# A hand-ordered transformer block on one core is replaced by one with a planned order, in which VectorE computes part of the softmax exponentials as sums of shifted bit patterns

## The chip, the cores and the metric

The kernel runs on one core of one Trainium2 chip. The metric is the device time of one execution in microseconds, the median over the runs. Engines are called as in the profile: PE (TensorE), ACT (ScalarE), DVE (VectorE), POOL (GpSimd) and SP (SyncE, which issues DMAs).

## The reference

One block on x of 2048 tokens and width D = 640, in bf16. `mod` is silu(c) times a matrix, cut into six vectors sa, ca, ga, sb, cb, gb.

```python
h = _layernorm(x) * (1 + ca) + sa
qkv = (h @ wqkv).reshape(B, S, 3, H, Dh)          # H = 32 heads, Dh = 20
scores = einsum('bhqd,bhkd->bhqk', q, k) * Dh ** (-0.5)
x = x + ga * ((softmax(scores) @ v) @ wo)
h = _layernorm(x) * (1 + cb) + sb
x = x + gb * (((h @ w_gate) * (h @ w_up)) @ w_down)   # inner width 1536
```

A unit below is the scores of one head for 128 keys and 512 queries, one 128x512 tile in a PSUM bank. There are 32 heads x 16 key tiles x 4 chunks of 512 queries = 2048 units.

## The kernel before

**Start** (lines 512 to 871). Modulation vectors are computed by matmuls, the layer norm of the four groups of 512 tokens runs on DVE with a square root on ACT, transposes on PE give hT, and ACT applies scale and shift while it evicts (L620). For each group the first half of V and the K of the first four heads are projected (`v_round`, `k_or_q_round`, evicted by DVE at L752 and L734). The other projections are left to rounds that are put between attention steps.

**Attention** (lines 1099 to 1221). Heads go in sets of three (ten sets, and one of two). An item is a chunk of queries with a set of heads, and has 16 steps, one for each key tile. A step is: one matmul of scores for each head, in the 32 rows of PE that hold that head (L1130); one exponential on ACT over all of them, 128x1536, into `Pbuf` (L1146); one PV matmul for each head, in its own 32 columns of PE (L1159), which sums over the 16 steps into PSUM bank 6. Column 0 of V is 1, so the sum of the exponentials comes out as a row of its own. Scores use two sets of three banks in turn, so the scores of step g + 2 wait for the exponential of step g. At the end of an item DVE transposes the sums (L1183), takes the reciprocal (L1187), multiplies (L1189) and transposes back into `Oc` (L1193). The next item's first PV waits for L1183.

**Order.** It is written by hand in a loop over 704 steps: exponential g, scores g + 2, PV g, and then `xs.inject(g)`, which puts a few matmuls of the waiting round (a projection or a piece of a suffix) behind them, up to a budget of time, into bank 7. Where there is none it puts a matmul that nobody reads (L852).

**Suffix** (`suffix_task`, from L915). For each chunk: out-projection over 11 sets of heads (L959) and the residual (L968), layer norm (L980 to L992), transposes (L999), gate and up projections (L1036, L1049) with DVE's product (L1054), the scaling of w_down by gb (L934), the down projection (L1073) and the result (L1083), stored by SP. The first three suffixes lie between the attention steps of the next chunks, and the fourth is the tail.

Of the kernel before, what the change touches and what calls it, by code (L numbers as in the profile page):

```python
# [4 lines left out]
ACT = mybir.ActivationFunctionType  # L5
# [4 lines left out]
F32R = mybir.dt.float32r  # L10

ENGS = ("sp", "act", "pe", "dve", "pool")


class Ev:
    __slots__ = ("ctr", "val", "step")

    def __init__(self, ctr, val, step=-10 ** 6):
        self.ctr = ctr
        self.val = val  # L20
        self.step = step


class Ctr:

    def __init__(self, prog, name, step=1):
        self.prog = prog
        self.name = name
        self.sem = prog.nc.alloc_semaphore(name)
        self.step = step  # L30
        self.n = 0
        self.owner = None


class EngProg:
    def __init__(self, prog, key):
        self.prog = prog
        self.key = key
        self.ops = []
        self.waited = {}  # L40

    def wait(self, *evs):
        for ev in evs:
            if ev is None:
                continue
            ctr = ev.ctr
            if ev.val > self.waited.get(ctr.name, 0):
                self.waited[ctr.name] = ev.val
                sem, val = ctr.sem, ev.val
                self.ops.append(lambda e, sem=sem, val=val: e.wait_ge(sem, val))  # L50

    def ins(self, fn, inc=None, waits=()):
        for ev in waits:
            self.wait(ev)
        ev = None
        if inc is not None:
            if inc.owner is None:
                inc.owner = self.key
            assert inc.owner == self.key, f"counter {inc.name} owned by {inc.owner}, used by {self.key}"
            inc.n += inc.step  # L60
            ev = Ev(inc, inc.n, self.prog.cur_step)
            sem, step = inc.sem, inc.step
            self.ops.append(lambda e, fn=fn, sem=sem, step=step: fn(e).then_inc(sem, step))
        else:
            self.ops.append(lambda e, fn=fn: fn(e))
        return ev


class Prog:
    def __init__(self, nc):  # L70
        self.nc = nc
        self.engs = {k: EngProg(self, k) for k in ENGS}
        self.ctrs = {}
        self.cur_step = -10 ** 6

    def ctr(self, name, step=1):
        assert name not in self.ctrs
        c = Ctr(self, name, step)
        self.ctrs[name] = c
        return c  # L80

    def __getitem__(self, k):
        return self.engs[k]

    def dgrp(self, name):
        return DmaGrp(self, name)

    def emit(self):
        nc = self.nc
        with nc.Block() as block:  # L90

            @block.sync
            def _(e):
                for f in self.engs["sp"].ops:
                    f(e)

            @block.scalar
            def _(e):
                for f in self.engs["act"].ops:
                    f(e)  # L100

            @block.tensor
            def _(e):
                for f in self.engs["pe"].ops:
                    f(e)

            @block.vector
            def _(e):
                for f in self.engs["dve"].ops:
                    f(e)  # L110

            @block.gpsimd
            def _(e):
                for f in self.engs["pool"].ops:
                    f(e)


class DmaGrp:

    def __init__(self, prog, name):  # L120
        self.prog = prog
        self.ctr = prog.ctr(name, 16)
        self.closed = False

    def dma(self, eng, fn, waits=()):
        assert not self.closed, "DMA group already closed"
        if self.ctr.owner is None:
            self.ctr.owner = eng.key
        assert self.ctr.owner == eng.key, "DMA group must use a single engine/queue"
        eng.ins(fn, inc=self.ctr, waits=waits)  # L130

    def done(self):
        self.closed = True
        return Ev(self.ctr, self.ctr.n)


class Arena:

    def __init__(self, nc, base, top):
        self.nc = nc  # L140
        self.base = base
        self.top = top
        self.cur = base
        self.peak = base
        self.count = 0

    def alloc(self, name, shape, dtype, align=64):
        size = 1
        for s in shape[1:]:
            size *= s  # L150
        size *= mybir.dt.size(dtype)
        off = (self.cur + align - 1) // align * align
        assert off + size <= self.top, f"SBUF overflow allocating {name} ({size} B at {off}, top {self.top})"
        self.count += 1
        t = self.nc.alloc_sbuf_tensor_at(f"{name}_{self.count}", list(shape), dtype, offset=off, align_bytes=32)
        self.cur = off + size
        self.peak = max(self.peak, self.cur)
        return t

    def mark(self):  # L160
        return self.cur

    def reset(self, m):
        self.cur = m

class Banks:

    def __init__(self, banks):
        self.banks = list(banks)
        self.free_ev = {b: None for b in self.banks}
        self.i = 0

    def next(self):
        b = self.banks[self.i % len(self.banks)]
        self.i += 1
        return b, self.free_ev[b]

    def release(self, b, ev):
        self.free_ev[b] = ev

    def set_all(self, ev):
        for b in self.banks:
            self.free_ev[b] = ev


class XRound:

    def __init__(self, mms, after, first_waits=(), name="", lag=2):
        self.mms = mms
        self.after = after
        self.first_waits = list(first_waits)
        self.name = name
        self.lag = lag

    def ready(self, step):
        for w in self.first_waits:
            ev = w() if callable(w) else w  # L200
            if ev is None:
                if callable(w):
                    return False
                continue
            if ev.step + self.lag > step:
                return False
        return True


class XTask:  # L210
    def __init__(self, name, ready_step, gen, budget=450):
        self.name = name
        self.ready_step = ready_step
        self.gen = gen
        self.done = False
        self.buf = None
        self.budget = budget

    def peek(self):
        if self.buf is None and not self.done:  # L220
            try:
                self.buf = next(self.gen)
            except StopIteration:
                self.done = True
        return self.buf

    def pop(self):
        r = self.peek()
        self.buf = None
        return r  # L230


class XSched:

    def __init__(self, pe, c_pe, banks, xbank):
        self.pe = pe
        self.c_pe = c_pe
        self.banks = banks
        self.xbank = xbank
        self.tasks = []  # L240
        self.cur = None
        self.round_end_step = -10
        self.no_start_until = -10
        self.xbank_free = None
        self.mode = "attn"
        self.stats = {"steps": 0, "mm": 0, "idle_steps": 0}
        self.filler = None
        self.filler_waits = []

    def add_task(self, task):  # L250
        self.tasks.append(task)

    def _head(self, step):
        while self.tasks:
            t = self.tasks[0]
            if step is not None and step < t.ready_step:
                return None
            if t.peek() is None and t.done:
                self.tasks.pop(0)
                continue  # L260
            return t
        return None

    def _issue_mm(self, rnd, i, bank, is_first):
        cost, fn = rnd.mms[i]
        last = (i == len(rnd.mms) - 1)
        waits = []
        if is_first:
            waits = [w() if callable(w) else w for w in rnd.first_waits]
            if self.mode == "attn":  # L270
                waits.append(self.xbank_free)
            else:
                waits.append(self.banks.free_ev[bank])
        ev = self.pe.ins(lambda e, fn=fn, bank=bank: fn(e, bank), inc=(self.c_pe if last else None), waits=waits)
        self.stats["mm"] += 1
        return ev, last
# [116 lines left out]
def build_kernel(nc, A_x, A_wqkv, A_wo, B_x, B_w_gate, B_w_up, B_w_down, c, w_mod, out,  # L393
# [4 lines left out]
    H = 32  # L398
# [889 lines left out]
```

## Time and profile before

| what | value |
|---|---|
| median of three runs | 1135.11 us (1135.11 to 1136.35) |
| span of the profiled execution | 1138.6 us |
| mean granted clock of PE | 0.913 of full speed |
| ACT busy | 969.7 us, 752 instructions |
| PE busy | 952.1 us, 6035 matmuls |
| DVE busy | 390.4 us, 690 instructions |

Rows of groups read: line, engine, operation, output and inputs, shapes, number; then busy time in us and mean length in ns; then the idle time of the engine before them and what ended it. Rows of a timeline begin with start and length in us, rows of the chain of waits too. Rows of stretches give the stretch, its length, the busy time of PE, PE's weight loads, DVE, ACT and POOL with numbers of instructions, the granted clock, the busy share of the DMA engines and GB/s.

### The profile page before, as it was taken

What the parts mean: (1) busy time and instruction counts of PE and PEld (TensorE: products, weight loads), DVE (VectorE), ACT (ScalarE), POOL (GpSimd) and SP (SyncE); (2) the same over time, 40 slices, a digit from 0 to 9 for tenths busy, and PEclk for the clock granted to TensorE, in tenths of its full rate; (3) what the DMA queues carried; (4) which work ended last, traced back from release to release, by engine and by line L of the source; (5) the groups of instructions that cost most, each with busy time, mean ns of one, the idle gap of its engine ahead of it and who ended that gap; (6) DMA issues with size and microseconds to landing.
All of it is one profiled execution on the core that took longest, in us unless ns stands there. A gap on an engine that the chain in (4) does not pass through costs nothing.

```text
span 1138.6 us, 14720 instructions
## 1 busy us (share of the span) xinstructions
PE 952.1 (84%) x6035; PEld 293.7 (26%) x6095; DVE 390.4 (34%) x690; ACT 969.7 (85%) x752; POOL 37.8 (3%) x52
## 2 busy tenths in 40 slices
PE   1677898899998888888997898889987888889778
PEld 0331222222222222222322222223222222223434
DVE  2741322344323333332114333321123333322475
ACT  1559999999999899999999999999987999999200
POOL 7000000000000000000000000000000000000000
PEclk9788999999989889898989779999977899989889
DMA  8100001000022001100230011100400011100422
GB/s 295 57 1 1 1 1 30 1 1 1 1 75 53 1 12 45 37 13 6 68 78 1 1 30 41 35 1 18 133 1 1 12 36 35 24 6 20 126 64 64
DMA packets 80418, 40.59 MB, mean 36 GB/s; under 512 B 64544, under 2 KB 80032, under 8 KB 80352
## 3 DMA queue, kind: packets, MB, share of 16 engines
q1 hardware_dynamic: 77328, 32.29, 11.0%
q10 hardware_dynamic: 2624, 4.92, 1.2%
q0 software_dynamic: 400, 2.46, 0.6%
q8 instruction: 48, 0.79, 0.3%
q14 instruction: 18, 0.15, 0.0%
HBM read 37.03 MB, written 2.62 MB: 35 GB/s over the span
## 4 chain that ended last, share of the span: by engine, by line
PE 39%; ACT 29%; issue 16%; DVE 13%; POOL 2%; another core or an unknown queue 0%; ACTq 0%; POOLq 0%
ACT Pbuf L1146 26%; PE ps_all L1159 9%; PE ps_all L1130 9%; PE ps_all L724 7%; PE ps_all L959 3%; PE ps_all L1036 3%; PE ps_all L1073 3%; PE ps_all L1049 2%; PE ps_all L746 2%; DVE OT L1183 2%; DVE KT_sb L734 1%; DVE QT_sb L734 1%; ACT hT L620 1%; PE ps_all L852 1%; DVE xn L990 1%
## 5 line engine op out<-in xcount | busy, mean ns | idle before, releaser
L1146 ACT ACTIVATE Pbuf<-ps_all 128x1536 bf16<-128x1536 f32 (+1 forms) x704 | 928.9, 1526 | 40.6 <-PE ps_all L1130 39.4
L1130 PE MATMUL ps_all<-QT_sb,KT_sb 32*128 32x512 bf16 x2048 | 296.1, 412 | 73.1 <-ACT Pbuf L1146 49.5
L1159 PE MATMUL ps_all<-Pbuf,V_sb 128*24 128x512 bf16 x2048 | 294.1, 412 | 9.0 <-DVE OT L1183 8.8
L1130 PEld LDWEIGHTS ps_all<-QT_sb,KT_sb 32*128 32x128 bf16 x2048 | 68.9, 92 | 323.7 <-ACT Pbuf L1146 244.2
L1159 PEld LDWEIGHTS ps_all<-Pbuf,V_sb 128*24 128x24 bf16 x2048 | 67.2, 89 | 189.4 <-issue 169.0
L959 PE MATMUL ps_all<-wo_sb,Oc 128*128 128x320 bf16 x352 | 76.7, 344 | 13.9 <-DVE h2T L1005 11.7
L1036 PE MATMUL ps_all<-h2T,wgst 128*128 128x512 bf16 x216 | 71.9, 410 | 9.8 <-DVE hprod L1054 4.4
L1073 PE MATMUL ps_all<-wd_sb,hprod 128*128 128x320 bf16 x384 | 72.5, 313 | 6.2 <-DVE wd_sb L934 5.4
L1049 PE MATMUL ps_all<-h2T,wust 128*128 128x512 bf16 x228 | 71.8, 398 | 4.9 <-DVE gsb L1041 3.4
L1183 DVE STREAM_TRANSPOSE OT<-ps_all 96x512 f32<-96x512 f32 (+1 forms) x44 | 31.3, 711 | 118.3 <-PE ps_all L1159 118.3
L1041 DVE COPY gsb<-ps_all 128x512 f32<-128x512 f32 x48 | 32.9, 685 | 89.8 <-PE ps_all L1036 82.4
L1054 DVE TENSOR_TENSOR hprod<-ps_all,gsb 128x512 bf16<-128x512 f32 x48 | 32.8, 684 | 89.9 <-PE ps_all L1049 78.8
L968 DVE TENSOR_TENSOR xck<-ps_all,xck 128x320 bf16<-128x320 f32 x32 | 15.3, 486 | 121.5 <-PE ps_all L959 121.5
L746 PE MATMUL ps_all<-Wv,hT 128*128 128x384 bf16 x160 | 40.6, 394 | 12.9 <-ACT hT L620 12.9
L1083 DVE TENSOR_TENSOR xck<-ps_all,xck 128x320 bf16<-128x320 f32 x32 | 15.5, 484 | 98.5 <-PE ps_all L1073 98.5
L724 PE MATMUL ps_all<-hT,Wk 128*128 128x512 bf16 x147 | 43.5, 394 | 6.3 <-DVE KT_sb L734 2.9
L724 PE MATMUL ps_all<-hT,Wq 128*128 128x512 bf16 x149 | 42.8, 383 | 5.3 <-issue 1.0
L734 DVE CAST KT_sb<-ps_all 128x512 bf16<-128x512 f32 x32 | 22.1, 691 | 67.1 <-PE ps_all L724 67.1
L959 PEld LDWEIGHTS ps_all<-wo_sb,Oc 128*128 128x128 bf16 x352 | 29.2, 106 | 51.8 <-issue 22.7
L734 DVE CAST QT_sb<-ps_all 128x512 bf16<-128x512 f32 x32 | 22.1, 692 | 56.0 <-PE ps_all L724 53.9
L1073 PEld LDWEIGHTS ps_all<-wd_sb,hprod 128*128 128x128 bf16 x384 | 30.3, 99 | 38.4 <-issue 17.9
L934 DVE TENSOR_TENSOR wd_sb<-wd_sb,mods_b 128x640 bf16<-128x640 bf16 x48 | 39.0, 813 | 0.0
(68 smaller groups left out, 433.5 us busy)
## 6 DMA issues: line engine op xcount, KB each, us to landing
wd_sb<-in_B_w_down_dram SPq DMA_DIRECT2D x4, 1920.0 KB, 9.4
wgst<-in_B_w_gate_dram SPq DMA_DIRECT2D x48, 160.0 KB, 2.7
wust<-in_B_w_up_dram SPq DMA_DIRECT2D x48, 160.0 KB, 2.8
wmod_sb<-in_w_mod_dram ACTq DMA_DIRECT2D x4, 1200.0 KB, 13.9
x<-in_A_x_dram SPq DMA_DIRECT2D x4, 640.0 KB, 7.1
xck<-in_A_x_dram SPq DMA_DIRECT2D x4, 640.0 KB, 4.3
out_dram<-xck SPq DMA_DIRECT2D x16, 160.0 KB, 1.8
wraw<-in_A_wqkv_dram POOLq DMA_DIRECT2D x5, 480.0 KB, 5.9
```

The lines of the kernel that those rows point to most:

```text
L724: fn = lambda e, b, kt=kt: e.matmul(psbank(b), Wx[:, kt, sg, :], hT[:, tc, kt, :], start=(kt == 0), stop=(kt == KT - 1))
L734: eve = dve.ins(lambda e: e.tensor_copy(dst[:, sg, tc * 512:(tc + 1) * 512], psbank(b)), inc=c_ev, waits=w)
L746: fn = lambda e, b, kt=kt: e.matmul(psbank(b)[:, 0:ncol], hT[:, tc, kt, (t % 4) * 128:(t % 4 + 1) * 128], Wv[:, kt, cc * ncol:(cc + 1) * n ...
L934: ev_wdp_l[0] = dve.ins(lambda e: e.tensor_tensor(wd_sb[:, fc, :], wd_sb[:, fc, :], mods_b[:, 2, :], ALU.mult), inc=c_ev, waits=[ev_wdl])
L959: fn = lambda e, b, j=j, tl=tl, nch=nch: e.matmul(ps_all[:, b, 0:320], Ocq[:, j, tl * 128:(tl + 1) * 128], wo_sb[:, j, nch * 320:(nch + 1) ...
L1036: fn = lambda e, b, kt=kt, stg=stg: e.matmul(psbank(b), wgst[:, stg, kt, :], h2T[:, kt, :], start=(kt == 0), stop=(kt == KT - 1))
L1049: fn = lambda e, b, kt=kt, stg=stg: e.matmul(psbank(b), wust[:, stg, kt, :], h2T[:, kt, :], start=(kt == 0), stop=(kt == KT - 1))
L1073: fn = lambda e, b, fc=fc, tl=tl, nch=nch: e.matmul(ps_all[:, b, 0:320], hprod[:, fc, tl * 128:(tl + 1) * 128], wd_sb[:, fc, nch * 320:(nc ...
L1130: fn = lambda e, bs=bs, i=i, sg=sg, s=s, cq=cq, kt=kt: e.matmul(ps_all[:, bs * 3 + i, :], KT_sb[32 * s:32 * s + 32, sg, kt * 128:(kt + 1) ...
L1146: fn = lambda e, sl=sl, nh=nh, bs=bs: e.activation(Pbuf[:, sl, 0:nh * 512], ps_sflat[bs][:, 0:nh * 512], ACT.Exp, scale=SCALE)
L1159: fn = lambda e, i=i, h=h, sl=sl, kt=kt: e.matmul(ps_all[32 * i:32 * i + VW, BO, :], V_sb[:, kt, h * VW:(h + 1) * VW], Pbuf[:, sl, i * 512 ...
L1183: ev_t1 = dve.ins(lambda e, rows=rows: e.transpose(OT[0:rows, :], ps_all[0:rows, BO, :]), inc=c_at, waits=[ev_pv[g], st["onorm"]] + extra)
```

## The change

The kernel is written anew. The program of each engine now comes from a planner (`Sched`) that runs when the kernel is built: each task has a duration, dependencies, a priority and buffer slots, the planner steps through a modelled time, and each engine's instructions stand in the order in which the planner started them. On the chip this order is fixed and only semaphores hold. The description calls it the same layout, but the kernel before has no such planner.

What is computed otherwise:

- Heads go in sets of four (8 sets), so an item has 64 units; 32 items in all. Scores use all four row groups of PE and PV all four column groups.
- ACT's units are cut into groups of three and two in turn, in banks 0 to 2 and 3 to 4. Banks 5 and 6 serve all other matmuls, bank 7 the PV sums.
- Of each item, 4 units in the first chunk and 8 in the others (`QUADS`) get no exponential on ACT. The queries are scaled at L750 so that a score is already 128 times the base-2 exponent. DVE adds a bias and clips at 0, written as int16 (L980); read as bf16, that is a piecewise linear exponential. Five more int16 tiles are made from it by adding a constant (L999, 2048 columns for four units). PE runs the PV matmul on each of the six tiles, so that their sum, with row sums that carry the same factor, stands for the exponential. The constants of ACT's exponential fit that factor.
- The start needs fewer modulation vectors: silu is computed with the exponential's table, and the two vectors of the first layer norm come as columns from 25 one-column matmuls each. Exponentials begin when the first keys are there. The out-projection packs the heads into 5 pieces of 128 rows, which SP copies together by DMA after each item (L1069). POOL scales wo and w_down.
- Where PE has little to do, the planner puts in matmuls that nobody reads (L1475).

The core of the diff:

```diff
+QUADS = [1, 2, 2, 2]
+SHIFTS = (0, 18, 34, 56, 77, 105)
...
-    SETS = [tuple(range(i, min(i + 3, H))) for i in range(0, H, 3)]
-    NSET = len(SETS)
-    VW = 24
+    NSET = 8
+    VW = DH + 1
...
+                u.is_d = q < nq and s == kg % 4
...
+        k = 3 if gi_ % 2 == 0 else 2
+        glist.append(ubuf[:k])
...
-        fn = lambda e, sl=sl, nh=nh, bs=bs: e.activation(Pbuf[:, sl, 0:nh * 512], ps_sflat[bs][:, 0:nh * 512],
-                                                         ACT.Exp, scale=SCALE)
-        ev_exp[g] = act.ins(fn, inc=c_exp, waits=waits)
+            return e.activation(pbuf[:, cellp["p"], 0:nu * 512],
+                                ps[:, b0:b0 + nu, :].rearrange("p b c -> p (b c)"), AFT.Exp, scale=ESCALE)
+        ta = Task("act", nu * 512 / 1.2 + 52.0, fexp, [ts], prio=g, name=f"E{g}")
...
+                return e.tensor_scalar(DB0[:, st_["slot"], x * 512:(x + 1) * 512], bank(cell["b"]), EBIAS, 0.0,
+                                       op0=ALU.add, op1=ALU.max)
...
+                return e.tensor_scalar(DSS[:, cell["s"], :], DB0[:, st_["slot"], :], float(SHIFTS[jj]), None, op0=ALU.add)
+            tsx = Task("dve", sb_cost(2048, .27), fsh, list(st_["p1"]) + wpad[("K", 1)] + wpad[("Q", 1)], prio=2.5 + .001 * qi, name=f"SH.{qi}.{jj}")
...
+                        srcf = lambda st_=st_, xx=xx: DB0[:, st_["slot"], xx * 512:(xx + 1) * 512].bitcast(BF16)
...
+                        srcf = lambda s_=st_["ss"][jj], xx=xx: DSS[:, s_, xx * 512:(xx + 1) * 512].bitcast(BF16)
...
+        d_xc = dma("sp", 128 * ntl * D * 2, lambda e: e.dma_start(xck[:, 0:ntl, :], xv[:, t0:t0 + ntl, :]),
+                   out_prev + proj_last, prio=15, gate=max(0, gb - 20))
```

How the order changes, at three places. PE, in the middle of an item of the second chunk, while the gate projection of the first is put between (QT and KT are queries and keys, Pbuf the exponentials, wgst the gate weights). Before:

```order
L1130 MATMUL ps_all<-QT_sb_86,KT_sb_85 128x512 x3
L1159 MATMUL ps_all<-Pbuf_78,V_sb_88 24x512 x3
L1036 MATMUL ps_all<-h2T_75,wgst_93 128x512
L1130 MATMUL ps_all<-QT_sb_86,KT_sb_85 128x512 x3
L1159 MATMUL ps_all<-Pbuf_78,V_sb_88 24x512 x3
L1049 MATMUL ps_all<-h2T_75,wust_94 128x512 x2
```

Now, in the last chunk (PA and PB are the exponentials of groups of three and two, DSS the shifted tiles, stg the gate and up weights):

```order
L919 MATMUL ps_all<-QT_73,KT_67 128x512 x3
L1307 MATMUL ps_all<-PA_78,Vf_77 21x512
L1307 MATMUL ps_all<-PA_78,Vf_77 32x512 x2
L1307 MATMUL ps_all<-DSS_81,Vf_77 32x512 x3
L1307 MATMUL ps_all<-DSS_81,Vf_77 21x512
L919 MATMUL ps_all<-QT_73,KT_67 128x512 x2
L1307 MATMUL ps_all<-PB_79,Vf_77 21x512
L1307 MATMUL ps_all<-PB_79,Vf_77 32x512
L1307 MATMUL ps_all<-DSS_81,Vf_77 32x512 x3
L1307 MATMUL ps_all<-DSS_81,Vf_77 21x512
L1191 MATMUL ps_all<-h2T_94,stg_99 128x512 x2
```

A phase of PV now holds the units of a group and four matmuls for one term of a quad, and a phase of PV or projections does not follow each phase of scores. DVE, at the end of an item with a suffix in the same stretch. Before (gsb and hprod are gate and product, OT to Oc the item's end):

```order
L1041 COPY gsb_76<-ps_all 128x512
L1183 STREAM_TRANSPOSE OT_79<-ps_all 96x512
L1187 RECIPROCAL invT_80<-OT_79 96x16
L1189 TENSOR_TENSOR OTn_81<-OT_79,invT_80 96x512
L1193 STREAM_TRANSPOSE Oc_35_83<-OTn_81 96x512
L1054 TENSOR_TENSOR hprod_77<-ps_all,gsb_76 128x512
L934 TENSOR_TENSOR wd_sb_92<-wd_sb_92,mods_b_53 128x640
```

Now:

```order
L1206 TENSOR_TENSOR hprod_93<-ps_all,gsb_101 128x512
L999 TENSOR_SCALAR DSS_81<-DB_32_80 128x2048
L1050 STREAM_TRANSPOSE OT_83<-ps_all 128x512
L999 TENSOR_SCALAR DSS_81<-DB_32_80 128x2048
L1053 RECIPROCAL invT_65<-OT_83 128x16
L999 TENSOR_SCALAR DSS_81<-DB_32_80 128x2048
L1055 TENSOR_TENSOR OTn_84<-OT_83,invT_65 128x512
L999 TENSOR_SCALAR DSS_81<-DB_32_80 128x2048
L1058 STREAM_TRANSPOSE OcT_85<-OTn_84 128x512
L999 TENSOR_SCALAR DSS_81<-DB_32_80 128x2048 x4
L980 TENSOR_SCALAR DB_32_80<-ps_all 128x512
```

The adds of 2048 columns stand between the steps of the item's end, and the scaling of w_down is gone from DVE. PE, behind the last exponentials (L1475 is read by nobody, wd and hprod belong to the third chunk, wo to the last). Before:

```order
L1159 MATMUL ps_all<-Pbuf_78,V_sb_88 24x512 x2
L852 MATMUL ps_all<-QT_sb_86,KT_sb_85 128x512
L959 MATMUL ps_all<-wo_sb_89,Oc_35_83 128x320 x44
L999 MATMUL ps_all<-ident_49,xn_22_70 128x128 x5
L959 MATMUL ps_all<-wo_sb_89,Oc_35_83 128x320 x22
```

Now:

```order
L1307 MATMUL ps_all<-PB_79,Vf_77 21x512
L1221 MATMUL ps_all<-wd_92,hprod_93 128x320 x74
L1475 MATMUL ps_all<-KT_67,ident_49 128x512 x12
L1119 MATMUL ps_all<-wo_98,Ocp_86 128x320 x40
L1475 MATMUL ps_all<-KT_67,ident_49 128x512 x6
L1151 MATMUL ps_all<-ident_49,xn_48_96 128x128 x20
```

The rest of the third chunk's down projection now stands between the last scores and the last out-projection, and the out-projection has 40 matmuls in one piece.

More of the change, by code (lines that the diff above doesn't have):

```diff
@@ L1 @@
 import math
+import heapq
 import concourse.bass as bass
 from concourse import mybir
-ACT = mybir.ActivationFunctionType
+AFT = mybir.ActivationFunctionType
 ALU = mybir.AluOpType
@@ L35 @@
[L35 to L44, printed above, removed]
-                continue
[L46 to L66, printed above, removed]
@@ L69 @@
[L69 to L115, printed above, removed]
@@ L118 @@
[L118 to L134, printed above, removed]
@@ L137 @@
[L137 to L164, printed above, removed]
@@ L210 @@
[L210 to L230, printed above, removed]
```

2261 lines of the change are left out of this document (1310 added, 951 removed).

## Prediction

> **What bounds the kernel now.** I read the page's head and slices, then the groups of instructions by form, then the timeline of the two ends and of one steady stretch, then the table of 40 us stretches.
>
> ```profile
> span 1138.6 us, 14720 instructions
> PE 952.1 (84%) x6035; PEld 293.7 (26%) x6095; DVE 390.4 (34%) x690; ACT 969.7 (85%) x752; POOL 37.8 (3%) x52
> ...
> PE   1677898899998888888997898889987888889778
> ...
> ACT  1559999999999899999999999999987999999200
> ```
>
> ScalarE (ACT) is full from the fourth slice to the 37th and empty at both ends; PE's 84% is pipelined matmuls with waits under them. The groups say what ACT does, and the timeline where it starts and stops:
>
> ```profile
> L1146 ACT ACTIVATE Pbuf<-ps_all 128x1536 bf16<-128x1536 f32 x640 | 869.6, 1570 | 37.5 <-PE ps_all L1130 36.7
> L1146 ACT ACTIVATE Pbuf<-ps_all 128x1024 bf16<-128x1024 f32 x64 | 61.4, 1093 | 3.1 <-PE ps_all L1130 2.7
> ```
>
> ```profile
> 91.41 4.13 ACT L1146 ACTIVATE Pbuf<-ps_all 128x1536 bf16<-128x1536 f32 x3
> ...
> 1029.67 31.24 ACT L1146 ACTIVATE Pbuf<-ps_all 128x1536 bf16<-128x1536 f32 x28
> ```
>
> The exponentials run from 91.4 to 1060.9 us. So the span is 91.4 of start, 969.5 of exponentials (931 busy by the two groups, 40.6 of waits for PE's scores) and 77.7 of tail. Inside the middle, PE keeps up:
>
> ```profile
> 500.49 0.39 PE L1130 MATMUL ps_all<-QT_sb,KT_sb 32*128 32x512 bf16 x3
> 500.81 0.39 PE L1159 MATMUL ps_all<-Pbuf,V_sb 128*24 128x512 bf16 x3
> 501.13 0.39 PE L1036 MATMUL ps_all<-h2T,wgst 128*128 128x512 bf16 x1
> 501.83 0.39 PE L1130 MATMUL ps_all<-QT_sb,KT_sb 32*128 32x512 bf16 x3 [0.31 <-ACT Pbuf L1146]
> ```
>
> ```profile
> 1099.18 1.08 PE ps_all L1036 x5
> 1122.66 13.21 PE ps_all L1073 x96
> ```
>
> One step is 1.34 us (500.49 to 501.83), ACT's pace. A phase of three tiled matmuls holds PE for 0.32 us. The last two rows, from the chain of waits in the tail, give 0.216 us for a 512-column matmul and 0.138 for a 320-column one; so 0.32 is one matmul time plus about 0.105 for the change of kind.
>
> **The exponentials.** The table QUADS takes 4 of 64 units in each of the eight items of the first chunk and 8 in the rest: 32 + 192 = 224 of 2048 units leave ACT, not an eighth. The order has 365 exponentials of three units, 364 of two and one of one. Priced by busy time per call (869.6/640 = 1.359, 61.4/64 = 0.959) they take 846 us. By distances from start to start, 1.34 above and 0.90 below, 818.
>
> The 0.90 is from the chain of waits, in the last item of two heads:
>
> ```profile
> 1055.24 0.69 ACT Pbuf L1146
> 1056.14 0.70 ACT Pbuf L1146
> ```
>
> I take 832 against 931: **99 us less**. One set of score banks is refilled while ACT reads the other; the shorter cover is now 0.9 us, which sufficed in the two-head steps of before (3.1 us of wait in 64).
>
> **The start.** Every item needs all 2048 keys. Before, projections of the four token groups came one after another, and no exponential ran until the first ones of all four were done. In the new order exponentials run on the keys at hand, and VectorE (DVE) sets when the last K tile of the first heads is there:
>
> ```profile
> L734 DVE CAST QT_sb<-ps_all 128x512 bf16<-128x512 f32 x32 | 22.1, 692 | 56.0 <-PE ps_all L724 53.9 <-remote 2.1
> L1083 DVE TENSOR_TENSOR xck<-ps_all,xck 128x320 bf16<-128x320 f32 x32 | 15.5, 484 | 98.5 <-PE ps_all L1073 98.5
> L568 DVE BATCH_NORM_STATS2 st<-x 128x6 f32<-128x320 bf16 x16 | 7.7, 483 | 11.2 <-DMA x<-in_A_x_dram 11.2
> L1005 DVE COPY h2T<-ps_all 128x640 bf16<-128x640 bf16 x16 | 7.8, 486 | 7.9 <-PE ps_all L999 7.9
> L988 DVE TENSOR_SCALAR xn<-xck,mv,rs 128x640 bf16<-128x640 bf16 x16 | 7.1, 446 | 16.0 <-POOL rs L985 16.0
> L1187 DVE RECIPROCAL invT<-OT 96x16 f32<-96x16 f32 x40 | 10.0, 249 | 1.4
> L690 ACT COPY Wk<-wraw 128x640 bf16<-128x640 bf16 x5 | 3.2, 724 | 7.8 <-DMA wraw<-in_A_wqkv_dram 7.8
> L934 DVE TENSOR_TENSOR wd_sb<-wd_sb,mods_b 128x640 bf16<-128x640 bf16 x48 | 39.0, 813 | 0.0
> ```
>
> Up to that K tile DVE's order holds 32 statistics x 0.483, 16 normalisations x 0.446, 18 evictions of transposes x 0.486, 12 of V x 0.484, 9 of 512 columns x 0.692, 5 shifts at 0.9 (below) and some 4 us of small ones: 52 us. The first x lands at 11.2 us as before; with about 5 us of waits for POOL and the modulation the tile is there at 68. The first exponential comes at about 33 us: x at 11.2, DVE's first statistics and normalisation 6, ACT's twelve copies of weights at 0.72 from 18 (L690's began at 30.3, behind 8.7 MB of loads; now some 5 MB lie ahead) to about 27, two projections of 2 and their evictions. By 68 us 44 of the first item's 60 ACT units can be done, 20 us of ACT at 0.456 a unit. So the start is worth 68 - 20 = 48 us instead of 91.4: **43 less** (between 36 and 51 less).
>
> **What is added to DVE.** Per four units: four evictions of 512 columns to int16 (0.692 each) and five adds over 2048 int16 columns. No row shows an int16 add in SBUF. Columns cost 1.08 ns and an instruction 0.14 us by the rows of 512 and 320 columns; L934's 640 columns fit that, the normalisation's 640 in 0.446 don't. With that row's rate and 0.14 fixed, 2048 columns take 1.1 us; with the small reciprocal's 0.249 as fixed cost, 0.9; at 1.08 ns a column, 2.35. I take 0.9, since the add has no per-partition operands to fetch: 10 adds and 8 evictions, 14.5 us per item, beside some 6 us of the item end, evictions and layer norm, about 20.5 of the 25.5 us in which ACT does 56 units. So DVE stays hidden.
>
> [...]
>
> **What is added to PE.** Six terms make 224 PV matmuls into 1344. Counted in the order: 3168 PV matmuls which, issued in order on four column groups, fill 951 slots x 0.216 = 205 us; 2048 scores in 183; 1812 others in 290 (K, V, out-projection use fewer or narrower matmuls: heads in fours, 21 columns of V, out-projection over 5 instead of 11 pieces); 1442 changes of kind x 0.105 = 151. That is 830; the same count of before, with 1992 changes, is 849. Longer PV phases thus pay for the six terms. Without tail (60) and what precedes the first score (5), 765 us lie beside some 890 us of exponentials and waits. PE is hidden at full clock, but tightly: in the first chunk it has as much work as ACT. So I take before's wait of 0.058 us a call (40.6/704) for 730 calls, 42, and 8 more for that chunk: **50**, between 15 and 110.
>
> ```profile
> 40.00:80.00 40.00, 27.02 (x164) 15.71 (x165) 24.46 (x67) 16.73 (x25) 2.41 (x1) 0.76 0.12 34
> 240.00:280.00 40.00, 36.83 (x243) 10.14 (x247) 19.44 (x29) 40.00 (x31) 0.00 (x0) 1.00 0.00 1
> 640.00:680.00 40.00, 35.04 (x201) 8.26 (x201) 13.40 (x23) 37.69 (x28) 0.79 (x2) 0.75 0.08 17
> ```
>
> ```profile
> core 0: 1138.6 us, clock 0.913
> ```
>
> The granted clock (third number from the end) is 1.00 where PE has projections between its phases and ACT is never idle, 0.75 where it has few. New PV phases are denser, so I expect at least 0.913, before's mean.
>
> **The tail.** SP stores the third chunk's output before it loads x for the last one into the same tile, and PE has 74 down-projections left when the last scores are gone.
>
> ```profile
> xck<-in_A_x_dram SPq DMA_DIRECT2D x4, 640.0 KB, 4.3
> out_dram<-xck SPq DMA_DIRECT2D x16, 160.0 KB, 1.8
> ```
>
> So: 1 for the last PV, 74 x 0.138 = 10.2, eviction 0.5, store 1.8, load 4.3: 17.8 us until the out-projection; the item end and its copies by DMA lie beside it. Then 12.5 for out-projection and layer norm (2 x 0.484, 2 x 0.483 and 0.446 of DVE per tile, four tiles, 3 to fill), 4 for transposes, 24 x 1.08 = 26, 13.2, and 3.3 for the last store: 77, as now. What the shorter out-projection wins, the late load takes.
>
> **Sum.** 48 + 832 + 50 + 77 = 1007 of span. Before's span of 1138.6 went with a median of 1135.11, so **1003 us**. Its own range is 955 to 1045.
>
> **Rivals.**
>
> *PE becomes the bound.* 555 of the 951 PV slots follow another in the same column group. If a weight load there isn't hidden, each adds its own time:
>
> ```profile
> L1159 PEld LDWEIGHTS ps_all<-Pbuf,V_sb 128*24 128x24 bf16 x2048 | 67.2, 89 | 189.4 <-issue 169.0 <-DVE OT L1183 19.0 <-DVE invT L1187 0.8
> ```
>
> 555 x 0.089 = 49, 814 in all, which at a clock of 0.913 take 892 us after the first exponential, at about 33 us; with 50 of waits, 33 + 892 + 50 + 77 = 1052 of span, 1048, and up to 1110 where the fixed order fits badly. For it: PE's tight sum. Against it: three PV matmuls with their loads share 0.32 us. [...]
>
> *DVE becomes the bound, and the kernel slower.* If the int16 add runs at 1.08 ns a column, an item holds 10 x 2.35 + 11.5 = 35 us of DVE, and 24 items take 840. With 48, 216 for the first chunk (27 an item, ACT's), 10 of waits and 77: 1191, 1188 measured. It decides from an add of 1.4 us on, and turns slower than now from about 2.1. For it: no row has an int16 operand. Against: the bf16 row runs at half that rate.
>
> *The planned order removes the waits too.* Waits of 10 and a start of 40: 955. Against: PE's order is fixed and its clock isn't.
>
> **How the numbers follow.** Forecast 0.60; PE bound 0.21; DVE bound 0.09; below 955 0.05; 0.05 for a static order that misses, split between 1110 to 1135 and slower. Range 955 to 1090: it takes in the forecast and most of the PE case and leaves out about 0.2. A measurement can tell 0.2% from no change. Faster 0.87, same 0.01, slower 0.12.
>
> **What would show it.** First exponential near 33 us, ACT gapless from about 68, last one near 930; the add at 0.7 to 1.1 us; wait before exponentials under 0.1 us a call. A DVE row of 2.3 us, or a PV phase growing by 0.3 us a slot, proves a rival. More than 110 us of waits, with neither, proves my 50 wrong.

## The result and the profile after

The changed kernel takes **1030.03 us** (median of 4 runs, 1028.66 to 1031.02) against 1135.26 before: a ratio of 0.907, 95% interval 0.906 to 0.9085. The forecast was 1003 us in a range of 955 to 1090. The page's head and slices of after:

```profile
span 1026.6 us, 16949 instructions
...
PE 940.6 (92%) x7028; PEld 296.3 (29%) x7028; DVE 598.8 (58%) x1055; ACT 856.0 (83%) x758; POOL 57.5 (6%) x69
...
PE   2799999999998999999999889999999999999888
...
ACT  3277999999797899989999989899899989999010
...
PEclk9899999999897898988899989989899979999989
```

ACT's row has dents all along, where before it was nearly all nines, and PE's row is now the fuller one. The groups of after, by form:

```profile
L944 ACT ACTIVATE PA<-ps_all 128x1536 bf16<-128x1536 f32 x365 | 538.9, 1476 | 64.9 <-PE ps_all L919 63.2
L944 ACT ACTIVATE PB<-ps_all 128x1024 bf16<-128x1024 f32 x364 | 382.9, 1052 | 19.1 <-PE ps_all L919 18.6
...
L999 DVE TENSOR_SCALAR DSS<-DB 128x2048 int16<-128x2048 int16 x280 | 184.6, 689 | 2.3 <-PE ps_all L1307 1.6
...
L980 DVE TENSOR_SCALAR DB<-ps_all 128x512 int16<-128x512 f32 x224 | 145.2, 683 | 21.4 <-PE ps_all L919 19.5
```

ACT waits 84.0 us (64.9 + 19.1) ahead of exponentials, nearly all for PE's scores. An add takes 0.689 us. The timeline of ACT in the start of after shows the calls that follow a wait:

```profile
30.29 1.45 ACT L944 ACTIVATE PA<-ps_all 128x1536 bf16<-128x1536 f32 x1 [5.13 <-PE ps_all L919]
...
50.59 1.45 ACT L944 ACTIVATE PA<-ps_all 128x1536 bf16<-128x1536 f32 x1 [15.67 <-PE ps_all L919]
...
63.55 1.02 ACT L944 ACTIVATE PB<-ps_all 128x1024 bf16<-128x1024 f32 x1 [4.73 <-PE ps_all L919]
...
73.39 1.02 ACT L944 ACTIVATE PB<-ps_all 128x1024 bf16<-128x1024 f32 x1 [2.96 <-PE ps_all L919]
...
86.67 1.45 ACT L944 ACTIVATE PA<-ps_all 128x1536 bf16<-128x1536 f32 x1 [5.45 <-PE ps_all L919]
```

I cut every span into the prediction's four terms. **Start** is the first exponential's time plus ACT's waits of over 1 us before exponentials up to 94 us; here 30.29 + 28.81 = 59.10 (the last four brackets). The first bracket, 5.13, lies before the first exponential, so it is in the 30.29 already. **Waits** are the rest of the 84.0: 84.02 - 28.81 - 5.13 = 50.08. The last exponential ends at 948.74, so **exponentials** are 948.74 - 59.10 - 50.08 = 839.56, and the **tail** is 77.9. Before, and the twelve experiments, in the same way (us; the clock is the mean granted one). The median of fill_small holds one execution in a slower state (1074.86 us); its other three took 1055.76 to 1066.71.

| kernel | start | exponentials | waits | tail | span | clock | median |
|---|---|---|---|---|---|---|---|
| before | 91.4 | 928.9 | 40.6 | 77.7 | 1138.6 | 0.913 | 1135.3 |
| after | 59.1 | 839.6 | 50.1 | 77.9 | 1026.6 | 0.928 | 1030.0 |
| q0_all_act | 44.7 | 930.3 | 14.4 | 68.3 | 1057.6 | 0.963 | 1055.3 |
| t3_terms | 56.2 | 836.6 | 34.1 | 68.8 | 995.7 | 0.937 | 997.3 |
| d_late | 55.9 | 837.8 | 46.0 | 86.1 | 1025.8 | 0.931 | 1029.1 |
| x_early | 59.0 | 839.6 | 50.0 | 68.4 | 1016.9 | 0.931 | 1019.9 |
| t3_five_adds | 56.5 | 843.0 | 55.8 | 112.4 | 1067.7 | 0.859 | 1071.8 |
| t3_three_quads | 56.2 | 795.0 | 36.4 | 119.4 | 1007.0 | 0.915 | 1010.2 |
| fill_first | 58.3 | 833.2 | 25.7 | 88.4 | 1005.7 | 0.981 | 1014.1 |
| t3_x_early | 55.5 | 837.3 | 39.6 | 68.7 | 1001.1 | 0.928 | 1000.7 |
| fill_small | 60.3 | 840.3 | 64.9 | 88.6 | 1054.0 | 0.921 | 1061.3 |
| evict_first | 61.5 | 833.6 | 23.8 | 71.4 | 990.4 | 0.972 | 991.3 |
| t3_fill_first | 61.4 | 833.8 | 21.7 | 68.7 | 985.6 | 0.971 | 987.6 |
| t3_fill_evict | 53.8 | 834.1 | 18.3 | 67.8 | 974.0 | 0.979 | 980.9 |

Four stretches of 40 us of after show where the waits behind the start lie:

```profile
160.00:200.00 40.00, 39.48 (x291) 11.33 (x291) 22.36 (x37) 39.97 (x36) 0.00 (x0) 1.00 0.01 3
...
320.00:360.00 40.00, 35.28 (x261) 8.81 (x258) 30.28 (x51) 31.87 (x27) 8.32 (x8) 0.76 0.02 5
...
480.00:520.00 40.00, 38.80 (x274) 11.12 (x273) 18.71 (x32) 34.96 (x31) 0.00 (x0) 0.84 0.16 32
...
880.00:920.00 40.00, 37.83 (x300) 10.37 (x294) 25.10 (x41) 40.00 (x36) 0.00 (x0) 1.00 0.16 36
```

In the two at a clock of 1.00 ACT (fourth busy time) is full. At 0.76 and 0.84 it lacks 8 and 5 us. Of the 20 stretches from 120 to 920 us, the eight with a clock of 0.99 or 1.00 hold 3.5 us of waits before exponentials, and the other twelve 46.

### The profile page after: what moved, and what is told of

Its sections match the earlier page's. It is cut to its first block, busy times and chain, and to the rows that moved or that the text cites. A ratio compares the mean times of both kernels' runs of the same rounds, so it can differ in the third digit from the quotient of the medians.

```text
span 1026.6 us, 16949 instructions
## 1 busy us (share of the span) xinstructions
PE 940.6 (92%) x7028; PEld 296.3 (29%) x7028; DVE 598.8 (58%) x1055; ACT 856.0 (83%) x758; POOL 57.5 (6%) x69
## 4 chain that ended last, share of the span: by engine, by line
PE 60%; DVE 18%; ACT 16%; issue 3%; POOL 1%; DMA 1%; ACTq 1%; DVEq 0%; POOLq 0%
PE ps_all L919 16%; PE ps_all L1307 13%; PE ps_all L1191 12%; ACT PA L944 9%; PE ps_all L738 8%; ACT PB L944 7%; DVE DSS L999 5%; PE ps_all L1221 4%; DVE DB L980 4%; PE ps_all L770 2%; PE ps_all L1119 2%; DVE st L657 1%; DVE OTn L1055 1%; DVE OT L1050 1%; DVE xck L1125 1%
## 5 line engine op out<-in xcount | busy, mean ns | idle before, releaser
L944 ACT ACTIVATE PA<-ps_all 128x1536 bf16<-128x1536 f32 x365 | 538.9, 1476 | 64.9 <-PE ps_all L919 63.2
L944 ACT ACTIVATE PB<-ps_all 128x1024 bf16<-128x1024 f32 x365 | 383.6, 1051 | 19.1 <-PE ps_all L919 18.6
L919 PE MATMUL ps_all<-QT,KT 32*128 32x512 bf16 x2048 | 347.9, 406 | 34.9 <-DVE DB L980 14.9
L999 DVE TENSOR_SCALAR DSS<-DB 128x2048 int16<-128x2048 int16 x280 | 184.6, 689 | 2.3 <-PE ps_all L1307 1.6
L919 PEld LDWEIGHTS ps_all<-QT,KT 32*128 32x128 bf16 x2048 | 83.5, 91 | 336.1 <-ACT PA L944 102.0
L1307 PE MATMUL ps_all<-PA,Vf 128*32 128x512 bf16 (+1 forms) x1095 | 165.9, 413 | 3.8 <-DVE OT L1050 3.7
L1307 PE MATMUL ps_all<-PB,Vf 128*32 128x512 bf16 (+1 forms) x729 | 160.5, 410 | 0.7 <-DVE OT L1050 0.4
L980 DVE TENSOR_SCALAR DB<-ps_all 128x512 int16<-128x512 f32 x224 | 145.2, 683 | 21.4 <-PE ps_all L919 19.5
L1307 PE MATMUL ps_all<-DSS,Vf 128*32 128x512 bf16 (+1 forms) x1120 | 146.7, 395 | 4.6 <-DVE DSS L999 4.5
L1191 PE MATMUL ps_all<-h2T,stg 128*128 128x512 bf16 x390 | 122.4, 420 | 0.5 <-DVE h2T L1156 0.3
L750 DVE TENSOR_SCALAR QT<-ps_all 128x512 bf16<-128x512 f32 x32 | 22.1, 690 | 39.2 <-PE ps_all L738 39.2
```

The costliest lines, as they stand in the source:

```text
L750: f = lambda e, ci=ci, so=so, n=n: e.tensor_scalar(QT[ci][:, j, :], ps[:, r.b["b"], so:so + n], QSCALE, None, op0=ALU.mult)
L919: ems.append(lambda e, i=i, kt=kt: e.matmul(dstf()[:, i * u.n:(i + 1) * u.n], KT[32 * u.s:32 * u.s + 32, u.j, kt * 128:(kt + 1) * 128], QT ...
L944: return e.activation(pbuf[:, cellp["p"], 0:nu * 512], ps[:, b0:b0 + nu, :].rearrange("p b c -> p (b c)"), AFT.Exp, scale=ESCALE)
L980: return e.tensor_scalar(DB0[:, st_["slot"], x * 512:(x + 1) * 512], bank(cell["b"]), EBIAS, 0.0, op0=ALU.add, op1=ALU.max)
L999: return e.tensor_scalar(DSS[:, cell["s"], :], DB0[:, st_["slot"], :], float(SHIFTS[jj]), None, op0=ALU.add)
L1191: f = lambda e, b, k=k, cell=wbuf[w_]: e.matmul(ps[:, b, 0:n], cell["t"][:, k, :], h2T[:, k, 0:n], start=(k == 0), stop=(k == KD - 1))
```

## The experiments

My theory, from the prediction: ACT's calls set the pace, so the gain is the start plus the exponentials that left ACT, and the remaining waits are PE's at a low clock. The rivals: the gain is the new layout's and order's, and the terms give back on PE what they save on ACT; PE is the bound throughout; VectorE's adds hold things up.

**q0_all_act: the layout without VectorE's exponentials.**

```diff
-QUADS = [1, 2, 2, 2]
+QUADS = [0, 0, 0, 0]
```

> All 2048 units of a head are exponentiated on ScalarE (QUADS is 0 for every chunk), so this run holds the new layout and order without the VectorE exponentials; nothing else is changed. Theory of the calls (mine): the gain of the change is the start plus the exponentials that left ScalarE. ScalarE then has 820 calls, 410 pairs at 2.25 us = 922 us in place of 834; start 55 to 59, waits 20 to 55, tail 78: span 1075 to 1114, measured about 1100. Theory of the layout: the gain is the new order's, and the six terms give back on TensorE (1120 more PV matmuls) what they save on ScalarE: 1020 to 1045.

Measured: 1055.31 us, a ratio to before of 0.927 (0.9245 to 0.930), between the two expectations. The groups of this run:

```profile
L944 ACT ACTIVATE PA<-ps_all 128x1536 bf16<-128x1536 f32 x410 | 657.7, 1604 | 29.5 <-PE ps_all L919 29.2
L944 ACT ACTIVATE PB<-ps_all 128x1024 bf16<-128x1024 f32 x409 | 483.7, 1183 | 5.0 <-PE ps_all L919 4.9
```

The 819 calls have nearly the price that I gave them (930.3 us without waits, 922 expected). But ACT waits 34.5 us instead of 84.0. So the layout alone wins 1138.6 - 1057.6 = 81 us of span: 46.7 in the start, 26.2 in waits and 9.4 in the tail, while the exponentials cost 1.4 more. Which of the layout's changes wins them, no run separates. VectorE's exponentials win 31 by these spans and 25 by the medians: they take 90.7 us from the exponentials and give back 14.4 in the start, 35.7 in waits and 9.6 in the tail. The theory of the calls falls as an account of the gain, and the rival of the layout is nearer the mark.

**t3_terms: three terms instead of six.**

```diff
-SHIFTS = (0, 18, 34, 56, 77, 105)
-SHIFT_GAIN = 3.046480226123085
+SHIFTS = (0, 43, 85)
+SHIFT_GAIN = 2.0011
```

> Three shifted terms (0, 43, 85) with their gain in place of six, so the VectorE exponentials are a coarser approximation; ScalarE's calls stay 730. It takes 672 of 3168 PV matmuls and 168 of 280 adds away; the matmul and phase count of TensorE's order falls from 830 to 790 us at full clock. If ScalarE's calls set the pace and the waits after the start (some 55 us) come from TensorE when its granted clock is low: waits 20 to 35, measured 1000 to 1015. If TensorE is the bound all along (the rival of the prediction): 40/0.93 = 43 less, 987 or below. If the waits have nothing to do with TensorE's load: 1025 to 1031.

Measured: 997.31 us, ratio 0.877 (0.874 to 0.880). That lies between the expected 1000 to 1015 and 987: the waits, 34.1, are in the expected 20 to 35, and the shorter tail was in neither sum. ACT has the same 730 calls and nearly the same time in them (836.6 us), and the kernel is 31 us of span shorter: 16 in waits, 9 in the tail, the rest in start and exponentials. So work taken from PE and DVE alone, with no call taken from ACT, wins most of what PE's order lost (40 us).

**t3_three_quads: more units leave ACT, PE's sum stays.**

```diff
-QUADS = [1, 2, 2, 2]
+QUADS = [1, 3, 3, 3]
...
-        return d_state[qi]["item"] <= st_pv["item"] + 1
+        return d_state[qi]["item"] <= st_pv["item"]
```

(with the three terms of t3_terms)

> Three terms and 12 instead of 8 units of an item on VectorE after the first chunk (QUADS 1, 3, 3, 3; a quad's scores come only in its own item's turn, which the longer list needs). 96 units more leave ScalarE, 43 us at 0.45 a unit, while TensorE's order keeps its sum (792 us at full clock, 790 in the run of three terms with two quads, 997.3 measured). If ScalarE sets the pace: 950 to 965. If TensorE does, exponentials that leave ScalarE win nothing: 990 to 1005, with ScalarE's waits some 40 us longer. Over 1005: the quads' own order costs.

Measured: 1010.17 us, ratio 0.889 (0.885 to 0.894). The exponentials fall by 41.6 us against t3_terms, as priced (43). The tail grows by 50.6, so it is the third expectation that came, over 1005. PE's timeline behind the last score:

```profile
898.01 28.52 PE L1191 MATMUL ps_all<-h2T,stg 128*128 128x512 bf16 x120 [0.99 <-DVE h2T L1156]
927.32 13.21 PE L1221 MATMUL ps_all<-wd,hprod 128*128 128x320 bf16 x96 [0.79 <-DVE hprod L1206]
...
947.00 7.28 PE L1119 MATMUL ps_all<-wo,Ocp 128*128 128x320 bf16 x40 [3.88 <-DMA xck<-in_A_x_dram]
```

The whole feed-forward of the third chunk is left over and runs after the attention, before the last chunk's out-projection. I had thought that ACT's waits would take the 41.6 us if PE is the bound. They grew by 2.3: PE's left-over work took them, in the tail. How much of that is the stricter turn for a quad's scores, the second line of the edit, this run doesn't tell.

**d_late: no VectorE units in the start.**

```diff
-            ts = Task("pe", 216.0, ems, list(dict.fromkeys(unit_score_deps(u))), ctr="pes", mode="S", name=f"D{qi}.{x}")
+            ts = Task("pe", 216.0, ems, list(dict.fromkeys(unit_score_deps(u) + (kt_ready[(0, 3)] if qi == 0 else []))), ctr="pes", mode="S", name=f"D{qi}.{x}")
```

> The first item's four VectorE units get their scores only when the fourth K tile is there, so VectorE has no shifted evictions and no adds between 33 and 72 us; nothing else is changed, the order behind it is planned anew. If the 11 us that the start came out longer than predicted lie in those four evictions and five adds (6 us of VectorE) ahead of the K tiles: third and fourth K tile 5 to 8 us earlier, measured 1020 to 1025. If the start is set by TensorE at half clock, by the loads or by the statistics: 1028 to 1031. A slower run (1033 or more) would say that the four postponed units cost more later than they win.

Measured: 1029.12 us, ratio 0.904 (0.901 to 0.907), no gain: the tiles come earlier as in the first expectation, and the time is that of the second. The fourth K tile is there at 65.8 instead of 72.2 us, but ACT's gap at the end of the first item grows from 5.45 to 8.69 us, since the put-off work lies there. The start wins 3.2, and the exponentials end 9.1 us earlier (939.65). The tail is 8.2 longer: 142 gate and up matmuls and 192 down-projections stand behind the last score, 120 and 174 in after. Again a gain on ACT came back as PE's left-over work.

**x_early: the last chunk's x in tiles of its own.**

```diff
+            d_x3 = dma("sp", 128 * 3 * D * 2, lambda e: e.dma_start(xl3[:, :, :], xv[:, t0:t0 + 3, :]),
+                       proj_last, prio=15, gate=int(gstart[NC] - 60))
+            d_xc = dma("sp", 128 * D * 2, lambda e: e.dma_start(xlast[:, :], xv[:, t0 + 3, :]),
+                       [d_x3] + proj_last, prio=15, gate=int(gstart[NC] - 60))
```

> The last chunk's x gets tiles of its own and is loaded well ahead, so its out-projection no longer waits for the third chunk's stores and the load behind them; TensorE's order is the same but for 12 fillers less. By the rows of the changed kernel (down-projections end at 959.4, out-projection begins at 966.3 behind the load): 6 to 7 us less, 1023 to 1024. If the copies of the last item's output are due next after the load: 0 to 3 less.

Measured: 1019.9 us, ratio 0.895 (0.891 to 0.8995), 10 us less where 6 to 7 were expected. PE's timeline behind the last scores, first of after, then of this run:

```profile
949.33 10.22 PE L1221 MATMUL ps_all<-wd,hprod 128*128 128x320 bf16 x74
...
959.39 2.75 PE L1475 MATMUL ps_all<-KT,ident 128*128 128x512 bf16 x12
...
966.26 7.28 PE L1119 MATMUL ps_all<-wo,Ocp 128*128 128x320 bf16 x40 [4.12 <-DMA xck<-in_A_x_dram]
```

```profile
949.18 10.22 PE L1231 MATMUL ps_all<-wd,hprod 128*128 128x320 bf16 x74
959.24 5.60 PE L1129 MATMUL ps_all<-wo,Ocp 128*128 128x320 bf16 x40
```

The out-projection begins 7.0 us earlier, as expected, and takes 5.60 us instead of 7.28: in after the granted clock was 0.50 from 967.5 to 970.9 us, behind PE's gap of 4.1 us, and here the 40 matmuls at 0.140 each keep the pace of the 74 of 320 columns above, 0.138 each at a clock of 1.00. Start, exponentials and waits are unchanged to 0.2 us: the tail's 9.5 is the whole gain of span.

**t3_x_early: both together.** The diffs of t3_terms and x_early in one kernel.

> Three terms (the same coarser approximation) and the early load of the last chunk's x together. The run of three terms had 997.3 and the early load alone won 10. If the two are independent: 987 to 990. In the run of three terms the tail was already 69 us instead of 78, so if that was the same gain: 995 to 998.

Measured: 1000.73 us, ratio 0.879 (0.876 to 0.883): nothing on top of three terms. There the third chunk's feed-forward is done before the last score (96 down-projections behind it, all of the last chunk), so the load was early already. PE's order holds as many matmuls as in t3_terms (6386), yet the clock is 0.928 instead of 0.937 and the waits are 5 us longer. So much comes with the clock in one and the same kernel: this run's four executions go from 995.55 us at a clock of 0.940 to 1002.9 at 0.928.

**t3_five_adds: PE's load of three terms, VectorE's of six.**

```diff
+        for jj in range(3):
...
+                return e.tensor_scalar(DSS[:, cell["s"], :], DB0[:, st_["slot"], :], 18.0, None, op0=ALU.add)
```

> Three terms as in the run of three terms (the same coarser approximation), but VectorE still makes five adds for every four units: three write shifted copies that nobody reads. So TensorE's load is that of three terms (767 us by the order at full clock, 790 in the run of three terms) and VectorE's that of six. If the 33 us that three terms won come from TensorE: 980 to 1005. If they come from VectorE's adds: 1020 to 1030.

Measured: 1071.79 us, ratio 0.943 (0.939 to 0.9465), 42 us more than the six terms and 74 more than the three; both expectations missed. PE's order is the lightest of all (767 us at full clock), but the clock is 0.859, and the third chunk's whole feed-forward lies in the tail (240 gate and up matmuls and 192 down-projections behind the last score). The adds stand ahead of the evictions in DVE's list, and fewer projections came between the attention steps. Whether DVE's time or the adds' hold on the three tiles for shifted copies did it, this run doesn't tell.

So two things came up together: projections that come late, and a low clock. Stretches of 10 us of after show the second:

```profile
250.00:260.00 10.00, 8.97 (x72) 2.42 (x71) 8.78 (x16) 8.23 (x9) 0.00 (x0) 1.00 0.01 2
260.00:270.00 10.00, 8.61 (x46) 1.50 (x44) 4.71 (x7) 8.15 (x7) 0.00 (x0) 0.55 0.03 9
...
330.00:340.00 10.00, 9.65 (x52) 1.53 (x46) 6.78 (x13) 8.43 (x8) 0.79 (x2) 0.50 0.00 0
```

PE is 86 and 97% busy in the last two (first busy time), at half its clock or little more. Projections (matmuls over all of PE) hold 1.98 us of the first stretch and 1.89 of the second, none of the ten us ahead of the third and 0.58 of it; in the five stretches from 200 to 250 us they hold 2.75 to 6.11 each, and the clock is 1.00. The rest are scores and PV, each matmul on a quarter of PE. Few projections don't lower the clock every time: from 290 to 300 us there are none, PE is 95% busy, and the clock is 1.00. From 100 to 900 us the clock stands at 0.50 in 17 stretches, 126 us together; PE is busy in 123 of them, and its longest idle time in all these 800 us is 2.2 us.

In the tail of after, a low clock follows idle time: the 3.4 us at 0.50 from 967.5 us on lie behind the gap of 4.1 us ahead of the out-projection. Ahead of the 17 stretches there is no such gap, since no idle time there is longer than 2.2 us.

**fill_first and fill_small: full-array work against the clock.** Matmuls that nobody reads, ahead of other work, and the same ones on a sixteenth of PE:

```diff
+        if 0 < pvstate["sidx"] < NG and sc.recent(t) < 3000 and t - last_fill[0] > 0 and fill_ok(t) and fill_now(t):
+            last_fill[0] = t
+            return True
```

```diff
-        task.emits = [lambda e: e.matmul(bank(b_), ident[:], KT[:, 0, 0:512])]
+        task.emits = [lambda e: e.matmul(bank(b_)[0:32, :], ident[0:32, 0:32], KT[0:32, 0, 0:512], tile_position=(0, 0))]
```

> Six terms as in the changed kernel. Fillers (512-column matmuls whose result nobody reads) are issued ahead of other work wherever the planner counts little full-array work in the last 3.4 us, instead of only when TensorE would idle: 130 instead of 28; TensorE's order grows from 830 to 865 us at full clock. If the low granted clock (0.50 to 0.67 in the stretches without projections) is what makes ScalarE wait, and full-array matmuls lift it: clock 0.97 or more, 1000 to 1020. If the clock has another cause, the 35 us come on top: 1045 to 1065.

> The order of fill_first word for word, all 130 fillers in their places, but each filler works on 32 rows and 32 columns of TensorE instead of 128 by 128 (still 512 columns of data, 0.216 us at full clock). If full-array activity holds the granted clock up, these fillers cost the same time and lift nothing: clock 0.93 or less, slower than fill_first's 1014 by 20 or more, 1035 to 1060. If fill_first's gain was its other order or the shifted tail: within 5 of 1014.

Measured: 1014.06 us, ratio 0.891 (0.886 to 0.896), and 1061.26 us, ratio 0.933 (0.926 to 0.939); by medians the first lies in the range expected of a clock that full-array work lifts, and the second 1 us above its range. Spans and clocks of the two:

```profile
core 0: 1005.7 us, clock 0.981
```

```profile
core 0: 1054.0 us, clock 0.921
```

The two have one order and differ only in how much of PE a filler uses; the clock and 48 us of span follow from that. So in these two runs the clock went with how much of PE a filler uses (0.981 with all of it, 0.921 with a sixteenth), and with the low clock ACT waits longer (64.9 us against 25.7). Whether it is the share of PE at work that counts or the tiled shape of a matmul, the two runs don't tell apart. Against after, PE does 35 us more of work and the kernel is 16 us faster.

**evict_first: VectorE's evictions ahead of its adds.**

```diff
-            tp = Task("dve", ps_cost(512), fp1, [ts] + wpad[("K", 1)] + wpad[("Q", 1)] + st_["p1"][:1], prio=3.0 + .001 * qi,
+            tp = Task("dve", ps_cost(512), fp1, [ts] + wpad[("K", 1)] + wpad[("Q", 1)] + st_["p1"][:1], prio=1.0 + .001 * qi,
```

> Six terms as in the changed kernel; in the planner's list VectorE's shifted evictions come before the adds of SBUF columns (priority 1.0 instead of 3.0), so that the two PSUM banks which VectorE's scores share with all projections come free earlier. TensorE's order holds 844 us at full clock instead of 830 (more changes of kind), and 107 instead of 174 down-projections behind the last score. If projections are held up behind VectorE's evictions: tail 68 to 72 instead of 78, the clock 0.94 or more, 1010 to 1022. If the 14 us more on TensorE decide: 1035 to 1045.

Measured: 991.31 us, ratio 0.871 (0.869 to 0.873), 39 us less than after by one number, with all six terms, and 19 better than the better expectation. Two of its stretches, as in after above:

```profile
320.00:360.00 40.00, 32.85 (x292) 9.61 (x284) 32.69 (x55) 34.72 (x32) 12.64 (x12) 0.91 0.05 12
...
480.00:520.00 40.00, 37.48 (x338) 11.96 (x336) 28.42 (x49) 39.81 (x36) 0.00 (x0) 1.00 0.22 54
```

The clock is 0.91 and 1.00 instead of 0.76 and 0.84. The records of projections and fillers are 1157 in the 810 us from 100 us on, and 1079 in 840 us of after: 1.43 a microsecond against 1.28. Banks 5 and 6 serve both VectorE's scores and all projections; with evictions first, more projections come between attention steps, the clock is higher, and fewer are left over (107 down-projections behind the last score instead of 174; tail 71.4). The gain is 26.2 us of waits, 6.0 of exponentials and 6.5 of tail, less 2.4 of start.

**t3_fill_first and t3_fill_evict: the causes combined.** Three terms with fill_first, and evict_first on top of both.

> Three terms (the same coarser approximation) and the fillers ahead of other work, both in one kernel; TensorE's order holds 831 us at full clock instead of 790, the tail's projections stay 49 us. If the clock is the cause of ScalarE's waits here too: clock 0.98, waits after the start 40 to 20 us, 975 to 985 against 997.3. If TensorE's 41 us more outweigh it: 1000 or more.

> Three terms (the same coarser approximation), fillers ahead of other work and evictions ahead of adds in one kernel. TensorE's order holds 825 us at full clock, its tail 49 us of projections. If low clock was all that was left of ScalarE's waits, and it is already gone in t3_fill_first (0.971, 987.6) and in evict_first (0.972, 991.3), nothing adds up: 980 to 988, the sum of start 61, exponentials 828, waits 22 to 30 and tail 69. If evictions first win through the banks as such, at any clock: 10 or more less, below 978.

Measured: 987.55 us, ratio 0.868 (0.866 to 0.870), and 980.87 us, ratio 0.864 (0.859 to 0.8695), the lowest median here, with the coarser approximation; the two intervals overlap. The first missed its 975 to 985 by 3 us, at a clock of 0.971 where I had put 0.98; the second lies in its 980 to 988. As expected of the second, the gains do not add: in the four runs with a clock of 0.971 to 0.981 the waits are 18 to 26 us, whichever way it got there. For six terms evict_first is the fastest; six terms with evictions first and an early x were not tried together.

## Why the prediction was right, and where it was off

The sum missed the median by 27 us: start +11.1, exponentials +7.6, waits +0.1, tail +0.9, and 6.9 because the median lies 3.4 above the profiled span, where I had put it 3.5 below as before.

**The start: the step that failed.** The first exponential came at 30.3 (forecast 33). K tiles of the first heads were evicted in after at:

```profile
49.41 0.68 DVE L746 CAST KT<-ps_all 128x512 bf16<-128x512 f32 x1
61.99 0.69 DVE L746 CAST KT<-ps_all 128x512 bf16<-128x512 f32 x1 [1.99 <-PE ps_all L738]
72.21 0.69 DVE L746 CAST KT<-ps_all 128x512 bf16<-128x512 f32 x1 [0.72 <-PE ps_all L738]
```

The fourth was there at 72.9 instead of 68, with 43 units done (44 forecast). About 5 us are that. Another 5.45 are the wait at the first item's end, which my sum stopped short of, and the rest is about 1 us. Without VectorE units the start is 44.7, so my 48 was nearly that of a kernel without them; d_late shows that putting them off doesn't help.

**Exponentials: right in size, wrong as a gain.** 839.6 against 832. But "99 us less" is the difference to before; against the same layout without them (q0_all_act) it is 90.7, of which 59.7 come back in the other terms. That the start, the waits and the tail depend on how many units leave ACT is the link that my sum lacked: it priced the terms one by one.

**DVE.** The add took 0.689 us where I took 0.9, so DVE's rival at 1.08 ns a column is out. My reason for the lower of two values, the missing per-partition operands, no run tests, and the 0.7 at which my range for the add began stands on no row of before. "DVE stays hidden" was true of its busy time (58%) and wrong of its order: with the evictions ahead of the adds the kernel is 39 us faster (evict_first), and the gain lies in ACT's waits for PE and in PE's tail.

**PE.** The measured 1030 lies closer to the PE rival's 1048 than to my 1003. Yet the rival's mechanism, a second weight load in one column group that isn't hidden, is out. PE's timeline of after, a phase of 11 PV matmuls, up to three in a column group, and the scores behind it:

```profile
143.48 0.39 PE L1307 MATMUL ps_all<-PA,Vf 128*32 128x512 bf16 x3
143.49 0.60 PE L1307 MATMUL ps_all<-DB,Vf 128*32 128x512 bf16 x4
143.72 0.59 PE L1307 MATMUL ps_all<-DSS,Vf 128*32 128x512 bf16 x4
144.24 0.39 PE L919 MATMUL ps_all<-QT,KT 32*128 32x512 bf16 x2
```

From 143.48 to 144.24 are 0.76 us, three slots of 0.216 and one change of 0.105; three slots with two loads of 0.089 would make 0.93. So the count of slots holds, and "hidden at full clock, but tightly" fits: eight stretches of 40 us at a clock of 0.99 or 1.00 hold 3.5 us of waits. What the rival had right is that PE's work costs time, in the waits and in the tail. What I had not worked out is that the tightness meets the clock.

**Waits.** 50.1 against 50, and that is luck: I had them from before's 0.058 us a call, and they go with PE's load and its clock. They are 14.4 us without the terms, 24 to 26 with evictions first or full-array fillers, and 64.9 with fillers on a small tile. I expected a clock of at least 0.913 because PV phases are denser. It was 0.928, but the reason was wrong: against the same layout without the terms (0.963) it fell.

**The tail.** 77.9 against 77, step by step: the 74 down-projections took 10.22 (10.2), and the out-projection began 17.5 us after the last exponential (17.8). That so much fits is in part the order, which I could count, but projections left over I did not see as a term that moves with the rest: the tail went from 67.8 to 119.4 in these runs.

Not settled: how much of evict_first's gain is the banks as such and how much the clock, since the plan is made anew with each edit and both move together. Nor what in t3_five_adds, VectorE's time or the adds' hold on the tiles, made the order so late.

## What to carry to other kernels

Price a change that moves work between engines against the new layout without it, not only against the old kernel: here 81 of the 112 us of span were the layout's. Where two engines are nearly full, as here (PE 92%, ACT 83% busy), work that leaves one can come back as the other's left-over at the end (the tail grew by 50.6 us in t3_three_quads), so count what stands behind the last instruction of the pacing engine. Among tiled matmuls the full-array ones kept the clock up here (0.981, against 0.921 for the same fillers on a sixteenth of PE), so spread them, and let the evictions of shared PSUM banks go before work that holds no bank (39 us less here).

## What was unexpected of the hardware

PE's granted clock was 0.50 in ten microseconds in which PE was 97% busy, nearly all of it with matmuls that each use a quarter of PE. 130 fillers of 512 columns held the mean at 0.981 when they used all of PE, and at 0.921 when they used 32 rows and 32 columns. An int16 add of 2048 columns in SBUF took 0.689 us, one of the shifted evictions from PSUM over 512 columns 0.683.
